# Three direct products for the first batch's maxout, the early loads in one sequence on GpSimd's queue, and a new instruction table

## Chip, core and metric

The kernel runs on one core of a Trainium2 chip. Its time is the device time in microseconds of that core, from launch to the last store. The profile's span is the time from the first to the last instruction of one profiled execution.

## The reference, cut to what matters

Eight batches, eight heads, 576 tokens, head size 64. Each head goes through linear attention with a feature map of 2 x 128 exponentials, and the heads' outputs, side by side, go through a feed-forward layer whose activation is the maximum of three products.

```python
def phi(x):
    proj = np.einsum('bhsd,df->bhsf', x, w_phi)
    proj = proj - np.max(np.abs(proj), axis=-1, keepdims=True)
    return np.concatenate([np.exp(proj), np.exp(-proj)], axis=-1)
q_p, k_p = (phi(q), phi(k))
kv = np.einsum('bhsf,bhsd->bhfd', k_p, v)
z = np.sum(k_p, axis=2)
num = np.einsum('bhsf,bhfd->bhsd', q_p, kv)
den = np.einsum('bhsf,bhf->bhs', q_p, z)[..., None] + 1e-06
x = (num / den)                       # then (tokens, 512)
h = np.maximum(np.maximum(x @ w1, x @ w2), x @ w3)    # 768 wide
out = h @ w_out
```

## The kernel before

**Attention** is cut into 16 units of four heads, two units to a batch, numbered 0 to 15 here. A unit's q and k stand side by side in a bf16 tile `qk_bf` and are transposed into `qkT` (18 tiles of 128 tokens), on TensorE for units 0 to 3 (line 490 for unit 0, line 493 for 1 to 3) and by a transposing DMA from unit 4 on. Then, per unit:

- five groups of projections on TensorE into `psq` and `psk` (L535, L530);
- for k: the exponentials `Ek` on ScalarE (L548), the row maxima `mk` on VectorE (L554), the factor `em` from the maxima (L585), and v times that factor, `vab` (L589), mostly on GpSimd; `kvps` (L643) is the product of the two;
- for q: the row maxima `mqp` on VectorE (L554). In units 0 and 1 the maximum is subtracted inside the product `psm` by small extra matmuls (L616, L619). From unit 2 on the maxima are transposed on TensorE (`pmT`, L562), copied to `mT` and written as one row into `qkT` by a small DMA (L570, from SP or from ScalarE's queue); the product `psm` (L614) waits for that row. The exponentials `Eq` follow on ScalarE (L627);
- `psn` (L661) is the product of `Eq` with the unit's k-v matrix, divided on VectorE (L667, L668) and turned into `xT` (on TensorE for units 0 and 1, L681; by a transposing DMA later).

**The feed-forward layer** takes 512 tokens of each batch as a chunk (chunks 0 to 7), and what is left of all batches as chunk 8. The maximum of three is rewritten: with the weight differences w2-w1 and w3-w1 (the "wd" steps, L785, on GpSimd) a chunk forms max(0, x(w2-w1), x(w3-w1)) from two sets of six `ups` products (four 128x512 matmuls each, L714), and adds x(w1 w_out) as "straight" products (four matmuls to a 128-token tile, L742) into the same accumulators as the down products (six matmuls, L747). w1 w_out is formed once from the transposed w1 (`pwT`, L797; `pm`, L811). The first `ups` set is copied out with a relu on ScalarE (L722) or VectorE (L724), the second is folded in by a maximum on VectorE (L720).

**What sets the order.** Each step is a node with one engine; a table `PLAN` of about 1,470 words fixes the order of the nodes, the engine of each and its buffer slots. A word such as `0G@0.7` is node 0, on GpSimd, ranked at 0.7. The engines run their instructions strictly in that order. The function `fill` puts idle products (`idler`, L842) on TensorE where the table leaves it free in the first stretch.

**Loads.** Unit 0's q and k come over SP's queue in fp32 halves and are cast on ScalarE (L447, L451). Units 1 to 3 take q and k by casting DMAs on GpSimd's queue (L458). The weights are on that queue too (L419), and v on either queue (L472). One-element copies (`gate`, L467) make a later load of v wait for a transposed tile of an earlier unit. A load on GpSimd's queue after the eighth waits for one that was issued eight earlier. `w_phi` is loaded twice, once to each half of the partitions (L360).

## Time and profile before

| | |
|---|---|
| median of 3 runs | 287.12 us (286.9 to 290.07) |
| span of the profiled execution | 285.3 us (no other time is given for it) |
| TensorE busy | 274.8 us, 96% |
| VectorE busy | 208.4 us, 73% |
| ScalarE busy | 192.5 us, 67% |
| GpSimd busy | 125.0 us, 44% |
| mean granted TensorE clock | 0.992 |

Busy shares are means over the whole span; the row of 40 slices and the view by windows show each stretch by itself. A busy TensorE counts a matmul from its start to its modelled end, so neighbours overlap; what a matmul costs in a dense row is the distance between starts. The median lies 1.8 us above the span.

### The profile page before, as it was taken

The page shows a single profiled execution, that of the slowest core. Times are in us where ns is not written, and L with a number is a line of the kernel's source. Part 1 is how long each engine was busy: PE and PEld are TensorE (multiplying, and loading weights), DVE is VectorE, ACT ScalarE, POOL GpSimd, SP SyncE. Part 2 cuts the span into 40 slices and gives each one's busy share as a digit, 9 for nine tenths or more (in the row PEclk, how much of TensorE's full clock was granted, in tenths as well). Part 3 has the DMA queues.
Part 4 walks back from the last instruction along what each step waited for, and adds up shares of the span by engine and source line. Part 5 has one row for each costly group of instructions (what it writes and reads, how often), then busy time and mean ns, then how long its engine had stood idle before and what let it go on. Part 6 is the DMA issues. An engine that isn't in the chain of part 4 may idle for free.

```text
span 285.3 us, 8441 instructions
## 1 busy us (share of the span) xinstructions
PE 274.8 (96%) x3485; PEld 155.7 (55%) x3522; DVE 208.4 (73%) x442; ACT 192.5 (67%) x445; POOL 125.0 (44%) x107
## 2 busy tenths in 40 slices
PE   8889999999999999999999999999999999999995
PEld 3557674565565555456565565555544664444442
DVE  2897899988999868688678779987975472227431
ACT  3798979997999987878868887779775400041001
POOL 9338999945923574417534950160080501000000
PEclk9997999999999999999999999999999999999999
DMA  7999979999899998988897998294420134153135
GB/s 192 203 284 262 312 144 305 341 239 250 221 293 196 225 232 280 251 156 202 258 251 272 268 199 182 99 182 81 82 62 3 27 54 90 37 110 76 37 85 173
DMA packets 67760, 51.46 MB, mean 180 GB/s; under 512 B 48778, under 2 KB 53002, under 8 KB 67722
## 3 DMA queue, kind: packets, MB, share of 16 engines
q1 hardware_dynamic: 62734, 43.38, 60.6%
q0 software_dynamic: 4576, 7.28, 12.1%
q8 instruction: 27, 0.44, 0.6%
q10 hardware_dynamic: 412, 0.28, 0.3%
q14 instruction: 11, 0.09, 0.1%
HBM read 34.67 MB, written 9.44 MB: 155 GB/s over the span
## 4 chain that ended last, share of the span: by engine, by line
PE 81%; DMA 8%; ACT 6%; POOL 1%; DVE 1%; issue 1%; ACTq 0%; POOLq 0%
PE ups L714 29%; PE ops L747 15%; PE ops L742 10%; PE psn L661 6%; PE kvps L643 6%; DMA qk_bf<-in_q_dram 5%; PE psm L614 5%; PE psq L535 4%; DMA qkT<-mT 3%; ACT Eq L627 3%; PE pm L811 2%; ACT Ek L548 2%; PE tps L493 1%; PE psq L530 1%; POOL qk_bf L458 1%
## 5 line engine op out<-in xcount | busy, mean ns | idle before, releaser
L714 PE MATMUL ups<-xT,w_bf 128*128 128x512 bf16 x415 | 101.5, 379 | 1.4 <-ACT Ek L548 0.5
L627 ACT ACTIVATE Eq<-psm 128x512 bf16<-128x512 f32 (+1 forms) x160 | 81.9, 582 | 15.6 <-PE psm L614 12.8
L589 POOL TENSOR_TENSOR vab<-v_raw,em 128x1152 bf16<-128x1152 f32 (+1 forms) x36 | 68.1, 1907 | 36.8 <-ACT em L585 27.9
L548 ACT ACTIVATE Ek<-psk 128x512 bf16<-128x512 f32 x128 | 73.5, 622 | 8.5 <-PE psk L535 5.8
L714 PEld LDWEIGHTS <-w_bf 128*128 128x128 bf16 x432 | 40.6, 98 | 45.4 <-issue 1.0
L720 DVE TENSOR_TENSOR hT<-hT,ups 128x512 bf16<-128x512 bf16 x54 | 36.4, 683 | 24.6 <-ACT hT L722 13.6
L554 DVE TENSOR_REDUCE mqp<-psq 128x4 bf16<-128x512 f32 (+1 forms) x80 | 49.0, 633 | 5.1 <-PE psk L535 2.9
L747 PE MATMUL ops<-wout_bf,hT 128*128 128x512 bf16 (+2 forms) x215 | 51.5, 373 | 0.5 <-issue 0.2
L554 DVE TENSOR_REDUCE mk<-psk 128x4 f32<-128x512 f32 x64 | 43.0, 683 | 0.7 <-PE psk L535 0.5
L747 PEld LDWEIGHTS <-hT 128*128 128x128 bf16 x222 | 21.1, 98 | 23.1
L668 DVE TENSOR_TENSOR x_sb<-psn,rden 128x320 bf16<-128x320 f32 x64 | 31.5, 492 | 2.2
L722 ACT ACTIVATE hT<-ups 128x512 bf16<-128x512 f32 x31 | 18.5, 615 | 21.1 <-PE ups L714 21.0
L755 ACT COPY osb<-ops 128x512 f32<-128x512 f32 (+2 forms) x17 | 9.6, 581 | 30.2 <-PE ops L747 12.7
L661 PEld LDWEIGHTS <-Eq 128*128 128x128 bf16 x640 | 24.9, 97 | 8.0
L755 DVE COPY osb<-ops 128x512 f32<-128x512 f32 x20 | 13.6, 689 | 20.1 <-PE ops L747 18.5
L661 PE MATMUL psn<-kv_sb,Eq 128*128 128x65 bf16 x640 | 26.8, 194 | 0.1
L742 PE MATMUL ops<-xT 128*128 128x512 bf16 x88 | 24.2, 379 | 0.4
L614 PE MATMUL psm<-qkT,wphi_m 128*128 128x512 bf16 (+1 forms) x70 | 22.3, 359 | 0.7 <-DMA qkT<-mT 0.6
L535 PE MATMUL psq<-w,qkT 64*128 64x128 bf16 x256 | 21.5, 217 | 0.5 <-DVE qkT L496 0.2
L476 POOL CAST qk_bf<-q_raw 128x1152 bf16<-128x1152 f32 x12 | 13.8, 1148 | 18.1 <-DMA q_raw<-in_q_dram 9.7
L535 PE MATMUL psk<-w,qkT 64*128 64x128 bf16 x256 | 21.3, 217 | 0.4 <-DVE mqp L554 0.4
L535 PEld LDWEIGHTS <-qkT 64*128 64x128 bf16 x512 | 14.8, 94 | 10.7 <-issue 8.1
(76 smaller groups left out, 272.6 us busy)
## 6 DMA issues: line engine op xcount, KB each, us to landing
out_dram<-osb SPq DMA_DIRECT2D x64, 128.0 KB, 2.5
v_raw<-in_v_dram SPq DMA_DIRECT2D x14, 576.0 KB
k_raw<-in_k_dram SPq DMA_DIRECT2D x11, 576.0 KB, 4.9
q_raw<-in_q_dram SPq DMA_DIRECT2D x11, 576.0 KB, 4.9
w_bf<-in_moe_w_dram POOLq DMA_DIRECT2D x3, 768.0 KB, 11.1
v_raw<-in_v_dram POOLq DMA_DIRECT2D x2, 576.0 KB, 13.7
qk_bf<-in_k_dram POOLq DMA_DIRECT2D x3, 288.0 KB, 13.4
qk_bf<-in_q_dram POOLq DMA_DIRECT2D x3, 288.0 KB, 13.6
```

Of the source, the lines that this page charges most:

```text
L535: nc.tensor.matmul(ps()[:, i, :], lhsT=cols[r, :], rhs=w2[r, c, :], start=True, stop=True)
L548: nc.scalar.activation(Ek[s]()[:, tiles_of(t0, n), :], of(1), EXP, scale=1.0 - 2.0 * s)
L554: nc.vector.tensor_reduce((mq, mk)[c]()[:, tiles_of(t0, n)], of(c), AXX, ALU.max, apply_absolute_value=True)
L589: (nc.vector if n_.eng == "DVE" else nc.gpsimd).tensor_tensor(vab()[:, g, t0:t1, 0:D], vb()[:, t0:t1, :], em()[:, g, t0:t1].unsqueeze(2).t ...
L614: nc.tensor.matmul(psm()[:, 0:w], lhsT=wphi_m, rhs=rhs, start=True, stop=True)
L627: nc.scalar.activation(Eqb()[s][:, cols], psm()[:, 0:w], EXP, scale=1.0 - 2.0 * s)
L661: nc.tensor.matmul(psn()[:, c, :], lhsT=Eqb()[g][:, t0:t0 + P], rhs=kv()[:, pr, ab, g, :], start=(g == 0), stop=(g == 1))
L668: nc.vector.tensor_tensor(x_sb()[:, pr, :, ab, :], psn()[:, :, 0:D], rden().to_broadcast([P, 5, D]), ALU.mult)
L714: nc.tensor.matmul(ups(), lhsT=w_bf[i + 1][:, ct, j * P:(j + 1) * P], rhs=tokens_of(ct), start=(ct == 0), stop=(ct == CT - 1))
L720: nc.vector.tensor_tensor(hT()[:, j, :], hT()[:, j, :], ups(), ALU.max)
L742: nc.tensor.matmul(ops_()[:, 0:width], lhsT=tile_of(ct, tt), rhs=line_w[c_i > MOVE][:, ct, cols], start=(ct == 0), stop=False)
L747: nc.tensor.matmul(ops_()[:, 0:width], lhsT=hT()[:, j, tt * P:(tt + 1) * P], rhs=wout_bf[:, j, cols], start=False, stop=(j == JT - 1))
```

## The change

Five edits, and a table that orders all steps anew.

1. **Chunk 0** takes the maximum of the three direct products x w1, x w2, x w3: eighteen `ups` products instead of twelve, the first six copied out without a relu, the other twelve folded in by a maximum. It has no straight products. The other chunks are as before.
2. **The weight differences** overwrite w2 and w3, so they now wait for chunk 0's products of the same columns, and the second copy of w1 w_out and the gathered last tokens, which overwrite w1, wait for all eighteen.
3. **The early loads** of q, k and v up to unit 3, and q and k of units 4 and 5, are all on GpSimd's queue, except unit 0's q, which stays on SP in two halves. Unit 0's k comes by two casting DMAs. Unit 0's `qk_bf` has the layout of units 1 to 3, so its 18 transposes become 36 half-height ones. The gates are gone.
4. **w_phi** is loaded by one transfer that reads it twice.
5. Some lists of buffers that only served the table lost entries.

The diff, without the table (one row of it stands for the rest):

```diff
-GATES = (None, (0, 0), (1, 0), (2, 0))
 PLAN = """
-0G@0.7 4A@0.7 6S0@0.7 2D0@0.8 3D@1.0 10S0@1.2 1G@1.3 12S@1.6 85G0@1.9 8S@2.1 84G@2.6 1075G@3.3 158G1@4.0 5D@4.1
+2D0@0.7 4A@0.7 6S0@0.7 10G0@0.7 3D@0.8 8S@1.1 83G1@1.4 0G@2.1 82G@2.7 11G@3.4 7D@3.7 1070G@4.2 5D@4.3 13T1@4.5 154G2@4.9
...
-    for ab in range(2):
-        nc.scalar.dma_start(wphi_f[ab * D:(ab + 1) * D, :], w_phi)
+    nc.scalar.dma_start(wphi_f, w_phi.unsqueeze(0).to_broadcast([2, D, DF]))
...
-        qk = buf("qk_bf", QK, [P, 2, UT, D] if by_pe and u else [P, UT, 2 * D], BF16)
+        qk = buf("qk_bf", QK, [P, 2, UT, D] if by_pe else [P, UT, 2 * D], BF16)
...
-                    if u == 0:
-                        def main(what=what, ts=ts, p0=p0, p1=p1, raw=raw):
-                            nc.sync.dma_start(by_pairs(raw()[:, ts, :]), rows_of(what, 0, p0, p1))
...
+                    if u == 0 and what == 0:
+                        def main(ts=ts, p0=p0, p1=p1, raw=raw):
+                            nc.sync.dma_start(by_pairs(raw()[:, ts, :]), rows_of(0, 0, p0, p1))
...
-                if by_pe and u < len(GATES) and GATES[u]:
-                    src, col = units[GATES[u][0]]["qkT"], BATCHES[GATES[u][1]][0] * P
-                    gates.append(nd("gate", {"DVE": 0.1}, lambda src=src, col=col, raw=raw: nc.vector.tensor_copy(
-                        raw()[0:1, 0, 0:1], src()[0:1, col:col + 1]), [], [src, raw]))
-                n_ = nd("Lv" if what == 2 else "L", {"SP": 0.62, "POOL": 0.75} if what < 2 and u <= AHEAD or u < 3 else {"SP": 0.62}, None, gates, [raw],
+                n_ = nd("Lv" if what == 2 else "L", {"POOL": 0.75} if u <= (3 if what == 2 else AHEAD) else {"SP": 0.62}, None, [], [raw],
...
-        for i in range(2):
+        direct = c_i == 0
+        for i in range(3 if direct else 2):
...
-                        nc.tensor.matmul(ups(), lhsT=w_bf[i + 1][:, ct, j * P:(j + 1) * P], rhs=tokens_of(ct),
+                        nc.tensor.matmul(ups(), lhsT=w_bf[i + (not direct)][:, ct, j * P:(j + 1) * P], rhs=tokens_of(ct),
...
-                a = ff(("up", "up2")[i], {"PE": 0.87}, up, ready + [diffs[i][j // 2]], [ups])
+                a = ff(("up", "up2", "up3")[i], {"PE": 0.87}, up, ready + [w_nodes[i] if direct else diffs[i][j // 2]], [ups])
+                if direct:
+                    firsts.append(a)
...
-                    if i == 1:
+                    if i > 0:
                         nc.vector.tensor_tensor(hT()[:, j, :], hT()[:, j, :], ups(), ALU.max)
+                    elif direct:
+                        copy_on[n_.eng](hT()[:, j, :], ups())
...
-                                         start=False, stop=(j == JT - 1))
-                n_s = ff("down", {"PE": 0.87 * width / DM}, straight, ready + lines[c_i > MOVE], [ops_])
+                                         start=(direct and j == 0), stop=(j == JT - 1))
+                n_s = []
+                if not direct:
+                    n_s.append(ff("down", {"PE": 0.87 * width / DM}, straight, ready + lines[c_i > MOVE], [ops_]))
...
+        if b == 1:
+            for i in range(2):
+                for h in range(JT // 2):
+                    diffs[i][h].deps += firsts[(i + 1) * JT + 2 * h:(i + 1) * JT + 2 * h + 2]
+            for n in lines[1]:
+                n.deps += firsts
```

Three places where the order moves. First, the head of GpSimd's queue. Before (the number after `qk_bf` tells the unit: 111 is unit 1, 126 unit 2, 226 unit 3; `k_raw` and `q_raw` here are unit 5's, `v_raw` unit 0's; w1, w2, w3 are `w0_bf`, `w1_bf`, `w2_bf`):

```order
L409 TENSOR_SCALAR minus_72<-ident_70 128x128
L458 DMA qk_bf_111<-in_k_dram 128x2x576
L458 DMA qk_bf_111<-in_q_dram 128x2x576
L419 DMA w0_bf_81<-in_moe_w1_dram 128x4x768
L458 DMA qk_bf_126<-in_k_dram 128x2x576
L458 DMA qk_bf_126<-in_q_dram 128x2x576
L472 DMA v_raw_142<-in_v_dram 128x2x576
L419 DMA wout_bf_84<-in_moe_w_out_dram 128x6x512
L419 DMA w1_bf_82<-in_moe_w2_dram 128x4x768
```

And now (89 is unit 0, 103 unit 1, 147 unit 2, 250 unit 3; `v_raw_180` is unit 0's, `v_raw_219` unit 1's):

```order
L453 DMA qk_bf_89<-in_k_dram 128x576
L453 DMA qk_bf_103<-in_k_dram 128x2x576
masks.py:197 MEMSET ident_69 128x128
masks.py:199 AFFINE_SELECT ident_69<-ident_69 128x128
L453 DMA qk_bf_103<-in_q_dram 128x2x576
L453 DMA qk_bf_89<-in_k_dram 128x576
L414 DMA w0_bf_80<-in_moe_w1_dram 128x4x768
L453 DMA qk_bf_147<-in_q_dram 128x2x576
L414 DMA wout_bf_83<-in_moe_w_out_dram 128x6x512
L462 DMA v_raw_180<-in_v_dram 128x2x576
L404 TENSOR_SCALAR minus_71<-ident_69 128x128
```

Unit 0's k moved here from SP's queue and stands first; the identity and its negative stand behind loads; w2 left the first eight.

Second, ScalarE ahead of chunk 0's first copy-out of `ups`. Before:

```order
L684 COPY xT<-pxT 128x576
L648 CAST kv_sb<-kvps 128x2x130
L815 CAST xT<-pm 128x512
L548 ACTIVATE Ek_721<-psq 128x2x128
L548 ACTIVATE Ek_764<-psk 128x512
L548 ACTIVATE Ek_721<-psk 128x512
L548 ACTIVATE Ek_764<-psq 128x2x128
L585 ACTIVATE em<-mk 128x18 x2
L599 CAST vab<-em 128x36
L548 ACTIVATE Ek_1092<-psk 128x512 x2
L548 ACTIVATE Ek_1106<-psk 128x512 x2
L722 ACTIVATE hT<-ups 128x512 x2
```

And now:

```order
L668 COPY xT<-pxT 128x576 x2
L806 CAST xT<-pm 128x512
L668 COPY xT<-pxT 128x576
L532 ACTIVATE Ek_897<-psk 128x512
L532 ACTIVATE Ek_904<-psq 128x2x128
L532 ACTIVATE Ek_904<-psk 128x512
L532 ACTIVATE Ek_1062<-psk 128x512 x2
L709 CAST hT<-ups 128x512
```

(721 and 764 are unit 2's two tiles of k exponentials before, 897 and 904 now; 1092 and 1106 unit 3's before, 1062 one of them now.) The copy-out now comes before the end of unit 2's exponentials and before unit 2's `em`.

Third, GpSimd between unit 1's `vab` and unit 2's. Before:

```order
L589 TENSOR_TENSOR vab<-v_raw,em 128x9x64 x4
L599 CAST vab<-em 128x2x9
L419 DMA w_bf<-in_moe_w_dram 128x4x768
L785 TENSOR_TENSOR w_bf<-w_bf 128x4x256 x2
L476 CAST qk_bf<-q_raw 128x18x64
L476 CAST qk_bf<-k_raw 128x18x64
L785 TENSOR_TENSOR w_bf<-w_bf 128x4x256
L589 TENSOR_TENSOR vab<-v_raw,em 128x18x64 x2
```

And now (the k load is unit 4's; the first weight load is w2, the second w3):

```order
L462 DMA k_raw_762<-in_k_dram 128x2x576
L414 DMA w1_bf_81<-in_moe_w2_dram 128x4x768
L466 CAST qk_bf_893<-k_raw_391 128x18x64
L462 DMA v_raw_918<-in_v_dram 128x2x576
L466 CAST qk_bf_989<-k_raw_762 128x18x64
L466 CAST qk_bf_989<-q_raw_275 128x18x64
L414 DMA w2_bf_82<-in_moe_w3_dram 128x4x768
L462 DMA v_raw_1064<-in_v_dram 128x2x576
```

The differences left this stretch, and the issue of w3 now stands behind the casts of units 5 and 4.

More of the change, by code (lines that the diff above doesn't have):

```diff
@@ L413 @@
     n_const = node("const", 0, {"DVE": 2.2}, zeros, [n_idle], [])
[L414 removed]
+    n_phi = node("phi", 0, {"ACT": 1.2}, lambda: None, [], [], pipe=0.05, lat=2.0)
     n_phi = node("phi", 0, {"DVE": 0.7}, phi_weights, [n_phi, n_const], [])
@@ L488, in tp @@
                     for n, t in enumerate(range(UT)[tiles_of(t0, nb)]):
-                        if u == 0:
-                            nc.tensor.transpose(tps()[:, n, :], qk()[:, t, :], ident)
-                            continue
                         for c in range(2):
@@ L502, in attention @@
                 tr[i] = c_
-            un["Tc"] = tr
-            for g in gates:
-                g.deps.append(units[GATES[u][0]]["Tc"][GATES[u][1]])
         else:
@@ L539, in attention @@
             a = nd("G", {"PE": 0.22 if n == 2 else 0.236 * len(part)}, lambda mms=mms: [f() for f in mms], [tr[ti], n_phi],
-                   [qkT, mk, mq] + tiles + Ek, mode=int(n == 4))
+                   [qkT] + tiles, mode=int(n == 4))
             projs.append(a)
@@ L644, in kmm @@
                                          start=(t + g == 0), stop=(t == UT - 1 and g == 1))
-        n_k = nd("K", {"PE": KPE}, kmm, exps + n_va, [vab, kv] + kvps + Ek, mode=1)
+        n_k = nd("K", {"PE": KPE}, kmm, exps + n_va, [vab] + kvps + Ek, mode=1)
         for ab in range(2):
@@ L831 @@
             x_last[b // 4][:, :, b % 4 * ST:(b % 4 + 1) * ST], xT[:, b, :, SM:SM + ST]),
-            units[2 * b]["done"] + units[2 * b + 1]["done"] + diffs[0] + diffs[1] + turned, []))
+            units[2 * b]["done"] + units[2 * b + 1]["done"] + diffs[0] + diffs[1] + turned + firsts, []))
     chunk(B, lasts, lambda ct: xT[:, :, ct, SM:SM + ST],
```

316 lines of the change are left out of this document (156 added, 160 removed).

## The prediction

> **What bounds the kernel now.** I read the page first: the busy shares, the 40 slices, the chain.
>
> ```profile
> span 285.3 us, 8441 instructions
> PE 274.8 (96%) x3485; PEld 155.7 (55%) x3522; DVE 208.4 (73%) x442; ACT 192.5 (67%) x445; POOL 125.0 (44%) x107
> PE   8889999999999999999999999999999999999995
> DVE  2897899988999868688678779987975472227431
> ACT  3798979997999987878868887779775400041001
> PE 81%; DMA 8%; ACT 6%; POOL 1%; DVE 1%; issue 1%; ACTq 0%; POOLq 0%
> ```
>
> TensorE is at nine tenths from the fourth slice on and holds 81% of the chain. VectorE and ScalarE are as full as it only in about the first 70 us. So two things count: how much TensorE has to do, and how late the first stretch hands it over. The chain puts chunk 0's first `ups` at 42.86 us, and gives the price of work in dense rows:
>
> ```profile
> 39.87 1.13 PE tps L493 x36
> 42.86 2.54 PE ups L714 x11
> 221.69 3.45 PE ups L714 x16
> 281.95 0.48 ACT osb L755
> ```
>
> A 128x512 product costs 3.45/16 = 0.216 us, a half-height transpose 1.13/36 = 0.031. With such prices for every form, the program's list up to 42.86 us is 25.1 us of work, so TensorE lost 17.7 us there (idle products included). What follows, up to the last product at 281.5, is 232.7 us of work in 238.7: only 6.0 us are lost after 42.86. The windows show who keeps TensorE waiting at first:
>
> ```profile
> 0.00:10.00 10.00, 7.92 (x47) 3.32 (x47) 3.86 (x16) 4.00 (x6) 7.65 (x16) 1.00 0.84 193
> 10.00:20.00 10.00, 8.78 (x160) 6.35 (x161) 9.27 (x21) 9.84 (x25) 2.86 (x5) 1.00 1.16 251
> 9.87:42.86 32.99, 30.94 (x603) 22.45 (x608) 29.57 (x66) 29.43 (x75) 24.08 (x22) 0.95 1.06 245
> 50.00:60.00 10.00, 9.90 (x131) 5.66 (x126) 9.63 (x20) 9.93 (x25) 9.95 (x8) 1.00 1.06 295
> ```
>
> Columns are TensorE, its weight loads, VectorE, ScalarE, GpSimd, granted clock, DMA share, GB/s. From the first exponential (9.87) to the first `ups` VectorE and ScalarE are busy 29.6 and 29.4 of 33.0 us: they set the pace there, and before 9.87 the loads do.
>
> **The change part by part.**
>
> *TensorE's work.* Chunk 0 gains 6 x 4 = 24 `ups` products and loses 4 x 4 = 16 straight ones: 8 x 0.216 = 1.73 us more. In the new order three groups of eight projections that stood ahead of the first `ups` stand behind it: 24 x about 0.03 (the price of the transposes, likewise half-height) = 0.72. So 2.45 us more lie behind the first `ups`. Unit 0's transposes: 36 x 0.031 = 1.1 instead of eighteen, of which eight took 0.61, below: equal.
>
> *The first exponential.* These rows lead up to it:
>
> ```profile
> 1.90 0.94 POOL L458 DMA_DIRECT2D qk_bf<-in_k_dram  x1
> 6.11 0.41 DVE L405 CAST w<-wphi_f 64x128 bf16<-64x128 f32 x1 [2.14 <-DMA wphi_f<-in_w_phi_dram]
> 6.50 0.61 PE L490 MATMUL tps<-ident,qk_bf 128*128 128x128 bf16 x8
> 8.32 1.29 DVE L554 TENSOR_REDUCE mqp<-psq 128x4 bf16<-128x512 f32 x2 [0.49 <-PE psq L535]
> 9.29 0.67 ACT L451 CAST qk_bf<-q_raw 128x576 bf16<-128x576 f32 x1 [0.98 <-DMA q_raw<-in_q_dram]
> 9.72 0.72 POOL L472 DMA_DIRECT2D k_raw<-in_k_dram  x1 [1.65 <-DMA qk_bf<-in_k_dram]
> 11.12 0.73 POOL L472 DMA_DIRECT2D q_raw<-in_q_dram  x1 [0.68 <-DMA qk_bf<-in_q_dram]
> 9.87 4.14 ACT L548 ACTIVATE Ek<-psk 128x512 bf16<-128x512 f32 x8
> ```
>
> ```profile
> q0 software_dynamic: 29, 0.03, 32.5%
> ```
>
> The last row is from the DMA view of the window 5 to 6 us: GpSimd's queue moved its first 29 packets there, and none in the window 0 to 5. The projections were there at 8.3; ScalarE was held by the casts until 9.9. Now everything hangs on unit 0's first half of k, first on GpSimd's queue. Its issue moves from 1.90 to where the identity was filled, 0.72: 1.2 earlier. The first casting load had landed by 9.72 at the latest, the next one 1.4 later, so half a load is 0.7 shorter: at the latest 9.72 - 1.2 - 0.7 = 7.8. Early end: first packet at 5.0 - 1.2, and 0.7 for half a load, 4.5. That queue shared the DMA engines with 1.15 MB on SP's, which is halved now, so I take a value between the ends, 6.5. From the transposes to the first reduction took 8.32 - 6.50 = 1.8, so the exponential comes at 8.4 (ends 6.4, if w_phi lands earlier than at 6.11 too, and 9.7): a gain of 1.4, between 0.2 and 3.4. The second half of q is now cast on ScalarE between exponentials, 0.67, counted below. One w_phi issue less, and the identity behind two issues (0.94 and 0.73), are covered: the table load and the wait for k.
>
> [...]
>
> *ScalarE and VectorE ahead of the first copy-out.* Their groups between 9.87 and 42.86, and from the page the product of two tiles on VectorE:
>
> ```profile
> L548 ACT ACTIVATE Ek<-psk 128x512 bf16<-128x512 f32 x26 | 14.3, 615 | 0.2 <-PE psk L535 0.2
> L554 DVE TENSOR_REDUCE mqp<-psq 128x4 bf16<-128x512 f32 (+1 forms) x14 | 8.4, 627 | 0.2 <-PE psk L535 0.2
> L815 ACT CAST xT<-pm 128x512 bf16<-128x512 f32 x4 | 2.4, 608 | 0.8 <-PE pm L811 0.8
> L684 ACT COPY xT<-pxT 128x576 bf16<-128x576 bf16 x2 | 1.3, 639 | 1.1 <-PE pxT L681 1.1
> ...
> L720 DVE TENSOR_TENSOR hT<-hT,ups 128x512 bf16<-128x512 bf16 x54 | 36.4, 683 | 24.6 <-ACT hT L722 13.6
> ```
>
> An exponential of 512 takes 14.3/26 = 0.55. Counted in the order up to the first `hT<-ups`, ScalarE has four large and two small exponentials fewer (2.2 + 0.8), one `pm` copy (0.6), two `em` and two small copies fewer (0.9); one `kv_sb`, one `pxT` copy and q's cast more (0.4 + 0.6 + 0.7): 2.8 less. VectorE has five large and three small reductions fewer (5 x 0.6 + 3 x 0.35), and `kv_sb`, `pxT`, `mT` and three gates (1.5); q's cast, one `pm` copy and two `vab` products more (0.5 + 0.6 + 1.3, priced as L720): 3.1 less. The two agree on about 2.7, if their idle time stays 3.4 us; 2.0 to 3.0 are the ends. The first `ups` then comes 1.4 + 2.7 = 4.1 earlier, at 38.8 (ends of the gain 2.2 and 6.4).
>
> *Loads behind that.* v of unit 0 has about the same bytes ahead of it as before. GpSimd issues six more loads, 6 x 0.73 = 4.4 us, with room for it (busy 2.86 of 10 us in 10 to 20). Without that cover unit 1's `vab`, its `kvps` and the first `ups` behind them come up to 4.4 later.
>
> *Six more maxima on VectorE* (0.68 each): 4.1 us, in a stretch where it is busy 9.63 of 10. TensorE has 1.73 us more work there; the rest could show, 0 to 2.3. I take 0.3, since reductions stood aside. The differences stay on GpSimd.
>
> *The row of maxima.* From unit 2 on TensorE transposes the maxima, works on, and then stops at `psm` if the row has not landed. By the order, the work between the two is 2.9 us in unit 7 and 3.9 or more elsewhere before; now it is 2.6, 2.7 and 2.6 in units 9, 11 and 13, 3.1 and 3.3 in 7 and 3, 3.7 in 2 and 12. What it takes:
>
> ```profile
> 111.68 0.22 PE L562 MATMUL pmT<-ident,mqp 128*128 128x128 bf16 x1
> 59.92 5.33 DMA qkT<-mT
> 112.22 3.42 DMA qkT<-mT
>   PE psm L614: 0.6, 2
> ```
>
> In unit 7 the row landed at 112.22 + 3.42 = 115.64, 3.96 after the transpose. The last row is from the view of the tile `mT`: two `psm` waited for the row, 0.6 us in all. At 3.96 each, the seven tight units would lose 1.3 + 1.3 + 1.4 + 0.9 + 0.7 + 0.3 + 0.3 = 6.2, less the 0.6 that is in the span already: +5.6. Where the queues are emptier the row needs less, and the loss may be nil: -0.6. Units 9 to 13 come after the first third, when fewer loads stand ahead, so I take +0.3.
>
> **The sum**: -4.1 + 2.45 + 0.3 + 0.3 = -1.05 us, a span of 284.2. The profiled span lies 1.8 under the median of the runs, so the time is 287.1 - 1.05 = 286.1. The difference is a third of a per cent, where a measurement of this kernel tells about 2% from no change.
>
> **The rivals.**
>
> *The whole gain arrives.* -6.4 + 2.45 - 0.6 = -4.55, 282.6. For it: TensorE loses 17.7 us before 42.86, and only there is much to win. Against it: it needs the early end of the load and of each wait. If half of ScalarE's and VectorE's remaining idle 3.4 us went as well, 280.9.
>
> *The row of maxima comes late on the strictly ordered TensorE*, the other side: with the middle start -4.1 + 2.45 + 5.6 = +3.95, 291.1; at worst -2.2 + 2.45 + 5.6 = +5.85, 293.0. It is one mechanism, seven places (`psm` of units 2, 3, 7, 9, 11, 12, 13). It decides once the row takes longer than 3 us from the transpose. For it: 5.33 and 3.42 us of DMA alone. Against it: these two had loads around them.
>
> *w3 lands late.* Its issue now stands behind the casts of unit 4's k and q on GpSimd. Before:
>
> ```profile
> 29.04 2.27 POOL L589 TENSOR_TENSOR vab<-v_raw,em 128x576 bf16<-128x576 f32 x2 [0.15 <-ACT em L585]
> 31.39 0.80 POOL L419 DMA_DIRECT2D w_bf<-in_moe_w_dram  x1
> 36.36 1.15 POOL L476 CAST qk_bf<-q_raw 128x1152 bf16<-128x1152 f32 x1
> w_bf<-in_moe_w_dram POOLq DMA_DIRECT2D x3, 768.0 KB, 11.1
> ```
>
> With unit 1's `vab` done at 31.3 again, two issues, a cast, an issue and two casts that wait for unit 4's k follow: issue at about 37 to 39, landing between 41 (a bare transfer of four) and 50 (the 11.1 us of the page's row). The first product with w3 stands 8.8 us of TensorE's work behind the first `ups`, at 47.6. Price 0 to 2.4: up to 288.5.
>
> *The first exponential does not move* (w_phi and k land as late as k did), and the rest holds: -0.2 - 2.7 + 2.45 + 0.6 = +0.15, 287.3.
>
> *The clock.* Where TensorE had little to do around 18 to 22 us, half the clock was granted:
>
> ```profile
> 20.00:22.00 2.00, 1.55 (x20) 1.12 (x20) 2.00 (x6) 2.00 (x6) 1.54 (x2) 0.88 1.17 269
> 22.00:24.00 2.00, 2.00 (x20) 1.36 (x20) 1.96 (x4) 0.93 (x3) 2.00 (x3) 0.50 1.21 209
> 24.00:26.00 2.00, 2.00 (x37) 1.55 (x33) 1.57 (x4) 1.82 (x6) 1.66 (x2) 0.76 1.16 211
> ```
>
> Now eight idle products instead of seventeen stand ahead of the first transposes. If they run out two us before k lands, the first groups go at half rate: their roughly 2 us of work doubles, +1.7 at most, 287.8. [...]
>
> **How the numbers follow.** Forecast (286.1): 0.36. Whole gain: 0.22. Row late: 0.20. w3 late: 0.12. First exponential unmoved: 0.05. Clock: 0.05. The forecast's own range, by half of each bound, is 284.0 to 288.2. The range for 8 in 10 reaches to 282.0, inside the whole-gain case, and to 291.0, half of the late row's cases. Faster by over 2% (under 281.4): 0.09 of the whole-gain case, where idle time goes too, and 0.03 of the forecast, 0.12. Slower by over 2% (over 292.9): 0.07 of the late row, 0.03 of w3 and of an uncovered GpSimd, 0.10. Within: 0.78.
>
> **What would show it.** First `Ek` at 8.0 to 9.0 and first `ups` at 38 to 40 would show the start right; a first `ups` at 41 or later, wrong. In the chain, `DMA qkT<-mT` at several of the seven units, with TensorE idle before `psm`, would show the late row. A TensorE wait for w_bf near 47 would show w3. Slices of PEclk under 9 in the first four would show the clock. The prediction is wrong if TensorE, after its first `ups`, loses more than 9 us or fewer than 4.

## The result and the profile after

The changed kernel takes 299.33 us (297.58 to 300.26) against 287.32 for the kernel before on the same chip: 1.0404 of it, 95% interval 1.0346 to 1.0462. It is slower. The forecast was 286.1 us, 282 to 291, with 0.78 for "within 2%". The ratios here and below come from undisturbed executions alone and the medians from all of them, so the two need not agree to the last microsecond.

From the page of the changed kernel's profiled execution (the second chain row gives shares by line, the last row is a group of instructions with its busy time, mean duration, and idle time before it with what ended it):

```profile
span 298.4 us, 8521 instructions
PE 280.6 (94%) x3540; PEld 156.6 (52%) x3540; DVE 211.7 (71%) x436; ACT 194.0 (65%) x449; POOL 128.1 (43%) x116
PE   6999999799979999699989979999999999999995
PEclk9999999799999999989999999999999999999999
PE 75%; DMA 13%; DVE 7%; ACT 2%; issue 1%; ACTq 0%; POOLq 0%
PE ups L699 27%; PE ops L736 14%; DMA qkT<-mT 9%; PE ops L731 8%; PE psn L645 6%; PE kvps L627 6%; PE psm L598 5%; PE psq L519 4%; DMA xT<-x_sb 2%; DVE mk L538 2%; DVE mqp L538 2%; DMA qk_bf<-in_k_dram 2%; ACT Ek L532 1%; PE tps L480 1%; PE idler L839 1%
L598 PE MATMUL psm<-qkT,wphi_m 128*128 128x512 bf16 (+1 forms) x70 | 22.1, 371 | 8.9 <-DMA qkT<-mT 8.9
```

DMA has gone from 8% of the chain to 13%, and 9% is one transfer, the row of maxima (`qkT<-mT`): TensorE idles 8.9 us ahead of `psm`, where it idled 0.7 before. In TensorE's row of slices there are now slices of 6 and 7 between the nines. The chain says where (start, duration, what):

```profile
40.18 4.32 PE ups L699 x20
48.91 4.98 DMA qkT<-mT
78.83 5.16 DMA qkT<-mT
84.80 5.37 DMA qkT<-mT
119.66 5.21 DMA qkT<-mT
150.83 3.34 DMA qkT<-mT
168.40 6.65 DMA xT<-x_sb
195.62 2.84 DMA qkT<-mT
```

These are the rows of units 2, 4, 5, 7, 9 and 12, from issue to landing, and one transposing DMA of x. The windows around the first of them (same columns as in the prediction's windows):

```profile
50.00:52.00 2.00, 1.75 (x9) 0.59 (x6) 1.82 (x5) 1.55 (x5) 2.00 (x2) 1.00 1.17 284
52.00:54.00 2.00, 0.06 (x1) 0.07 (x2) 0.21 (x1) 0.64 (x2) 2.00 (x2) 0.98 1.05 387
54.00:56.00 2.00, 2.00 (x5) 0.67 (x6) 0.00 (x0) 1.09 (x2) 0.89 (x1) 0.50 0.29 103
```

TensorE stands still from 51.8 to 53.9 while the DMA engines are full, and once it may go on it runs at half clock: the trace grants 0.5 from 53.90 to 57.31, and again from 125.58 to 128.99 behind unit 7's row.

**Where the 13.1 us went** (298.4 - 285.3), in the prediction's own accounts: the first `ups` is at 40.0 instead of 42.86, -2.8; by the prediction's count 2.45 more TensorE work stands behind it; and behind it TensorE loses 294.8 - 40.0 - 235.2 = 19.6 us instead of 6.0, +13.6; the end behind the last product is 0.2 shorter. These 13.6 are the rows' waits, 8.9 - 0.6 = 8.3; one wait for xT, 1.9; and two windows of 3.41 us at half clock, counted at half of their length each, 3.4. The kernel before also had 0.7 us of other waits behind its first `ups`, and these are gone; so 0.7 of the 13.6 has no place in this list, and the work may have grown by more than the count.

### The profile page after: what moved, and what is told of

It is laid out like the page before. It is cut to its first block, busy times and chain, and to the rows that moved or that the text cites. A ratio compares the mean times of both kernels' runs of the same rounds, so it can differ in the third digit from the quotient of the medians.

```text
span 298.4 us, 8521 instructions
## 1 busy us (share of the span) xinstructions
PE 280.6 (94%) x3540; PEld 156.6 (52%) x3540; DVE 211.7 (71%) x436; ACT 194.0 (65%) x449; POOL 128.1 (43%) x116
## 4 chain that ended last, share of the span: by engine, by line
PE 75%; DMA 13%; DVE 7%; ACT 2%; issue 1%; ACTq 0%; POOLq 0%
PE ups L699 27%; PE ops L736 14%; DMA qkT<-mT 9%; PE ops L731 8%; PE psn L645 6%; PE kvps L627 6%; PE psm L598 5%; PE psq L519 4%; DMA xT<-x_sb 2%; DVE mk L538 2%; DVE mqp L538 2%; DMA qk_bf<-in_k_dram 2%; ACT Ek L532 1%; PE tps L480 1%; PE idler L839 1%
## 5 line engine op out<-in xcount | busy, mean ns | idle before, releaser
L699 PE MATMUL ups<-xT,w_bf 128*128 128x512 bf16 x456 | 107.5, 382 | 2.0 <-DMA xT<-x_sb 1.9
L611 ACT ACTIVATE Eq<-psm 128x512 bf16<-128x512 f32 (+1 forms) x160 | 79.1, 582 | 22.0 <-PE psm L598 21.1
L573 POOL TENSOR_TENSOR vab<-v_raw,em 128x1152 bf16<-128x1152 f32 (+1 forms) x34 | 65.7, 1949 | 44.4 <-ACT em L569 28.7
L699 PEld LDWEIGHTS <-w_bf 128*128 128x128 bf16 x456 | 43.2, 98 | 50.2 <-issue 3.8
L707 DVE TENSOR_TENSOR hT<-hT,ups 128x512 bf16<-128x512 bf16 x60 | 39.7, 683 | 16.4 <-PE ups L699 15.5
L746 ACT COPY osb<-ops 128x512 f32<-128x512 f32 (+2 forms) x24 | 13.7, 585 | 30.4 <-issue 16.2
L713 DVE TENSOR_SCALAR hT<-ups 128x512 bf16<-128x512 f32 x25 | 16.8, 687 | 16.3 <-PE ups L699 16.3
L711 ACT ACTIVATE hT<-ups 128x512 bf16<-128x512 f32 x23 | 13.9, 613 | 19.5 <-PE ups L699 19.4
L627 PE MATMUL kvps<-vab,Ek 64*128 64x65 bf16 x1152 | 21.0, 192 | 0.6 <-DVE xT L806 0.3
L731 PE MATMUL ops<-xT 128*128 128x512 bf16 x80 | 21.3, 392 | 0.0
```

What stands on the lines that cost most here:

```text
L573: (nc.vector if n_.eng == "DVE" else nc.gpsimd).tensor_tensor(vab()[:, g, t0:t1, 0:D], vb()[:, t0:t1, :], em()[:, g, t0:t1].unsqueeze(2).t ...
L611: nc.scalar.activation(Eqb()[s][:, cols], psm()[:, 0:w], EXP, scale=1.0 - 2.0 * s)
L627: nc.tensor.matmul(kvps[ab]()[:, t // NT, g, :], lhsT=Ek[g]()[r, t, :], rhs=vab()[r, g, t, :], start=(t + g == 0), stop=(t == UT - 1 and g ...
L699: nc.tensor.matmul(ups(), lhsT=w_bf[i + (not direct)][:, ct, j * P:(j + 1) * P], rhs=tokens_of(ct), start=(ct == 0), stop=(ct == CT - 1))
L707: nc.vector.tensor_tensor(hT()[:, j, :], hT()[:, j, :], ups(), ALU.max)
L731: nc.tensor.matmul(ops_()[:, 0:width], lhsT=tile_of(ct, tt), rhs=line_w[c_i > MOVE][:, ct, cols], start=(ct == 0), stop=False)
```

## Experiments: the rows of maxima

All times below, but for one that rests on a single execution, are medians of four runs or more, with the ratio to the kernel before on the same chip and its 95% interval. Unless another base is named, an edit is to the changed kernel.

**The control.**

> The changed kernel once more, unaltered, on the chip on which the next three run, so that they have it beside them. Both theories: 1.035 to 1.046 of the kernel before, with the same stalls at psm (about 8 to 11 us together, units 2, 4, 5, 7 the longest).

299.4 us, 1.0473 (1.0438 to 1.0509). The waits for the row were 6.3 us here, and another 1.2 ahead of a `psm` was put down to VectorE; in this execution w3 was late too:

```profile
51.34 0.61 PE L699 MATMUL ups<-xT,w_bf 128*128 128x512 bf16 x2 [1.03 <-DMA w_bf<-in_moe_w_dram]
```

The total repeats; which DMA is the late one differs from one execution to the next.

**Nobody waits for the row.**

```diff
-                qkT()[D:D + 1, :].rearrange("o (t c) -> o t c", c=P), mT())
+                aside[0:UT, :], mT())
```

> The changed kernel, but the row of maxima goes to a small tile of its own, and psm does not wait for it (the subtraction of the maxima is left out from unit 2 on). Theory A (the row comes late on the strictly ordered TensorE): the six stalls of psm, 9.85 us in the changed kernel's trace, go, and with them the two half-clock windows behind the longest of them, 2 x 3.41 us at half rate, some 3.5 us: 299.3 - 13.4 = 286, between 285 and 289, and TensorE loses under 8 us after its first ups. Rival B (the stalls only stand where another shortage shows first, of VectorE, ScalarE or transposing DMAs): under 5 us come back, 294 or more, with new waits ahead of the exponentials or of ups.

294.2 us, 1.033 (1.0254 to 1.0405). This kernel leaves out the subtraction of the maxima from unit 2 on. The stalls at `psm` are gone (0.1 us left in the group), and the traced execution has a span of 289.7, 8.7 under the changed kernel's; but it was the shortest of the four: by the medians 5 us came back and by the ratios 2 to 4, not 13. Theory A's mechanism stood, its sum did not. Rival B was right on the size, but the new waits are no engine's. The view of TensorE's waits (total, times, longest):

```profile
PE ups L700 <- DMA xT<-x_sb: 2.9, 2, 2.7
PE psq L520 <- DMA qkT<-qk_bf: 1.1, 1, 1.1
```

They are other DMAs: the transposing DMA of x at 165.5 us, with a half-clock window of its own behind it (165.86 to 169.28), and the transposing DMA of unit 5's q and k at 63.

**The same in the kernel before.**

> The kernel before with the row of maxima in a tile of its own for which nobody waits (the subtraction of the maxima is left out from unit 2 on). If the order before had the cover that the change lost, the row costs it next to nothing: 0.6 us of waits for the tile mT in its trace, so 0.995 to 1.0 of the kernel before. If rows cost it more than its trace shows (late exponentials behind them), 0.985 to 0.994.

284.75 us, 0.9958 (0.9939 to 0.9977). In the old order the row cost 1.2 us, in the new one 2 to 5. The row is the same transfer in both; what differs is when it is issued, what moves beside it, and how much TensorE work stands between the transpose of the maxima and `psm` (its cover).

**psm moved back in the order.** In the table's order the six units' `psm` and exponentials get 1.4 to 2.9 us on their start, and whatever depends on them or takes their buffers next is moved behind them. The edit also lets no new idle products in behind 13 us; the trace has the same twenty as the changed kernel's.

```diff
+    later = {2: 2.7, 4: 2.2, 5: 1.4, 7: 2.9, 9: 1.6, 12: 1.4}
...
+        if n.kind in ("M", "eq") and n.u in later:
+            n.start += later[n.u]
```

> The changed kernel with the psm products of the six units that stalled (2, 4, 5, 7, 9, 12) and their exponentials 1.4 to 2.9 us later in the order, so that other products stand between the transpose of the maxima and psm; nothing is left out, and the rows' DMAs are as they were. Theory A (what was lost is the cover between transpose and psm): most of the 9.85 us of stalls and the 3.5 of half clock go; 13.4 at best, some of it given back where numerators and x come later: 287 to 292. Rival B (the rows are late because the DMA engines are full, and what comes behind psm is as short of cover): the stalls move to psn or ups, under 4 us gained, 295 or more.

320.1 us, 1.1201 (1.1151 to 1.1251): 20 us worse, which neither theory had. Against the changed kernel's trace the span is 21.2 us longer; TensorE's waits behind the first `ups` grew from 10.8 to 22.8 us, and 20.5 us there are at half clock instead of 6.8. The waits:

```profile
PE psn L668 <- ACT Eq L634: 4.3, 6, 1.4
PE psm L621 <- ACT Eq L634: 3.4, 3, 2.7
PE psk L542 <- ACT Eq L634: 3.1, 3, 1.9
```

TensorE waits for the delayed exponentials of q (`Eq`), 15.5 us in all, and for the row only 0.7: `psn` needs their results, `psm` and `psk` the buffers that they free. Cover was not had here by pushing one step back: the step's followers need the kernel's same eight `bank` buffers and the same ScalarE.

**Every row from SyncE's queue.**

```diff
+        if n.kind == "V":
+            n.eng = "SP"
```

> The changed kernel with every row of maxima issued from SyncE's queue; five were issued from ScalarE's (units 2, 4, 5, 6, 7: 4.98, 5.16, 5.37, 1.90, 5.20 us from issue to landing, against 1.93 to 3.60 from SyncE's). Theory A1 (the rows wait behind loads and transposes at the DMA engines, whatever queue issues them): rows of units 2, 4, 5, 7 still take 4 us or more, time within 2 us of the changed kernel's, 297 to 301. Theory A2 (it is ScalarE's queue that is served late): they take 2 to 3.5 us, the stalls of these four units (7.8 us) and the half-clock windows (3.5) go: 288 to 291.

307.35 us, 1.065 (1.057 to 1.0731), the wrong side of both theories. Unit 2's row took 4.94 us from this queue as well, so the queue is not what makes it long. Units 4, 5 and 7 took 3.4 to 4.5, but those of 2, 4 and 7 were issued 1.7 to 3.2 us later behind their transposes:

```profile
116.78 7.66 SPq L495 DMA_TRANSPOSE qkT<-qk_bf  x1
127.89 0.81 SPq L557 DMA_DIRECT2D qkT<-mT  x1
L601 PE MATMUL psm<-qkT,wphi_m 128*128 128x512 bf16 (+1 forms) x70 | 22.5, 377 | 13.1 <-DMA qkT<-mT 13.1
```

The issue of a transposing DMA held SyncE for 7.66 us, until 124.44; then four more issues stood ahead of unit 7's row, which was transposed at 124.18, issued at 127.89 and landed at 131.26.

**What makes a row long.** The DMA view between issue and landing in the changed kernel, of the rows of units 2, 5, 7 and, last, 6:

```profile
DMA packets 2224, 1.58 MB, mean 315 GB/s; under 512 B 1761, under 2 KB 1761, under 8 KB 2224
DMA packets 997, 2.12 MB, mean 392 GB/s; under 512 B 87, under 2 KB 87, under 8 KB 996
DMA packets 2615, 1.15 MB, mean 222 GB/s; under 512 B 2379, under 2 KB 2379, under 8 KB 2614
DMA packets 128, 0.03 MB, mean 16 GB/s; under 512 B 128, under 2 KB 128, under 8 KB 128
```

The first three took 4.98, 5.37 and 5.21 us, the last 1.90. Large loads (unit 5) and the many small packets of a transposing DMA (unit 7) do it alike. In the first 4.0 us behind the issue of unit 2's row no packet of ScalarE's queue starts, and then all 27 do within 0.1 us; in units 5 and 7 the first starts after 4.0 and 4.3 us, in unit 6 after 1.4, and only unit 4's are spread, from 2.0 to 4.6. The row's first completion, 1.1 to 1.8 us after the issue in all fourteen, comes ahead of its packets in these five and says nothing of its data. So these rows were late to begin, not slow to move: but for unit 4's, all 27 packets of a row started within 0.9 us. The next experiment takes the loads away from ahead of three rows:

```diff
+        if n.kind == "V" and n.u in (2, 4, 5):
+            n.eng = "SP"
+        if n.eng == "SP" and n.kind in ("L", "Lv"):
+            for a, row in ((39.0, 45.2), (69.9, 70.8), (71.0, 75.3)):
+                if a < n.start < row:
+                    n.start = row + 0.01 * (1 + n.start - a)
```

> The changed kernel with the rows of units 2, 4 and 5 on SyncE's queue and the loads of k, q and v that stood just ahead of them there moved behind them (two ahead of unit 2's row, one ahead of unit 4's, three ahead of unit 5's). In the changed kernel 1.56, 1.58 and 2.11 MB were moved between the issue of these rows and their landing, 4.98, 5.16 and 5.37 us; unit 6's row, with 0.02 MB beside it, took 1.90. If the bytes ahead of a row set its length, the three take 2 to 3 us, their stalls (2.35, 1.88, 1.04 us) fall under 0.5 each and the half-clock window behind the first (1.7 us) goes: 5 to 6 us less, 293 to 295. If loads that come later make units late instead, TensorE waits for transposing DMAs (qkT<-qk_bf) and the time is 297 or more with rows as short.

296.2 us, 1.0282 (1.0208 to 1.0357). The three rows took 2.04, 2.23 and 2.07 us instead of 4.98, 5.16 and 5.37, and their stalls are gone; beside unit 4's 0.61 MB were moved instead of 1.60. On SyncE's queue with the loads still ahead the same rows had taken 4.94, 3.87 and 4.52: here it was the bytes ahead that made these rows long, not the queue. The time fell by 3 us by the medians and 5 by the ratios. Both branches of the expectation came true in part, since other DMAs are now late (TensorE's waits):

```profile
PE psq L527 <- DMA qkT<-qk_bf: 1.7, 1, 1.7
PE ups L707 <- DMA xT<-x_sb: 1.6, 2, 0.9
PE psm L606 <- DMA qkT<-mT: 1.4, 3, 0.6
```

The same kernel on another chip:

> The kernel with rows first once more, unaltered, on the chip of the next two. Where it is the DMAs that land at other times from one execution to the next, it is again between 1.02 and 1.036 of the kernel before, with rows of 2 to 2.3 us in units 2, 4 and 5 and TensorE waiting for other DMAs (unit 5's transposing DMA at 65 us, xT at 106 and 167).

296.66 us, 1.0352 (1.0288 to 1.0416); rows of 3.12, 2.24 and 1.93 us, and 2.5 us of waiting for unit 5's transposing DMA, but none for xT. By this one rows first gains 1.5 to 3.5 us, depending on which ratio of the changed kernel it is held against. The waits change places again.

## Experiments: what else is late

**w3 earlier on GpSimd's queue.**

```diff
+        if n.kind == "W" and n.u == 2:
+            n.start = 29.25
```

> The changed kernel with w3's load issued on GpSimd's queue right behind w2's, ahead of the casts of unit 4; in the changed kernel it was issued at 38.42, as the transposing DMA of unit 4 began, which took SyncE 9.26 us instead of 2.80, and as unit 2's row was to go. If w3 beside the transposing DMA is what delays unit 2's row (4.98 us), that row lands in 2 to 3 us, the stall of 2.35 us and the half-clock window behind it (1.7 us) go, and the time falls by 3 to 4, 295 to 296. If not (the row is late through its queue or the other loads), the stall at psm of unit 2 stays over 1.5 us and the time within 1 us of 299.3.

299.47 us, 1.0386 (1.0281 to 1.0492): nothing gained. Unit 2's row did take 2.83 us and did not stop TensorE, as the first branch had it; the 2.8 us that TensorE was ahead at 60 us were all but gone at 90:

```profile
PE psm L602 <- DMA qkT<-mT: 7.8, 5, 3.1
PE psq L523 <- DMA qkT<-qk_bf: 1.8, 1, 1.8
```

Unit 5's transposing DMA stopped it at 66.2, and the rows of units 5 and 7 took 6.37 and 5.99 us.

**The weight differences left out**, with the row aside. A guess of mine was that GpSimd, where 12.7 us of differences now stand behind 51 us instead of ahead of 52, hands over its casts late.

```diff
-            n_ = node("wd", 0, {"DVE": 1.2, "POOL": 2.1}, None, [w_nodes[0], w_nodes[i + 1]], [])
-            n_.fn = lambda n_=n_, f=diff: f(n_)
+            n_ = node("wd", 0, {"DVE": 1.2, "POOL": 2.1}, lambda: None, [w_nodes[0], w_nodes[i + 1]], [])
```

> As the kernel with the row aside (nobody waits for the row of maxima, their subtraction is left out from unit 2 on), and the six weight differences on GpSimd (2.1 us each, 12.7 us, since the change behind chunk 0's products instead of between 32 and 52 us) are left out too. With the row aside the time was 1.033 of the kernel before, and TensorE then waited for a transposing DMA at 63 us (1.28), vab of GpSimd at 149.7 (0.97), xT at 165.5 (2.88 and a half-clock window). If the late differences hold up GpSimd's casts and with them the transposing DMAs, the first of these goes and the time falls by 2 to 4 us against the row aside: 1.02 to 1.026. If not, it stays within 1 us of it, and what is left of the loss lies in xT and in small waits.

297.2 us, 1.0318 (1.0231 to 1.0405), as with the row aside alone. The guess falls: without any differences unit 5's transposing DMA was as late.

```profile
PE psq L520 <- DMA qkT<-qk_bf: 2.1, 1, 2.1
```

**Loads behind unit 5's transposing DMA**, on top of rows first:

```diff
-            for a, row in ((39.0, 45.2), (69.9, 70.8), (71.0, 75.3)):
+            for a, row in ((39.0, 45.2), (50.0, 51.8), (69.9, 70.8), (71.0, 75.3)):
```

> The kernel with rows first, and the two loads ahead of unit 5's transposing DMA on SyncE's queue (1.15 MB) moved behind it. In the kernel with rows first TensorE waited 1.84 us for that DMA at 65 us. If it lands late because of the loads ahead of it, the wait falls under 0.5, and the time by 1 to 2 us against rows first (by 3 in executions with a half-clock window behind it). If the transposes themselves take that long, or the x of units 2 and 3 behind them come late instead, it is within 1 us.

294.4 us, 1.0287 (1.0224 to 1.035), 2.3 us under rows first on the same chip, though the intervals overlap. The wait at 65 us is gone, as expected. What is left in the traced execution:

```profile
PE ups L707 <- DMA xT<-x_sb: 4.3, 3, 2.2
PE psm L606 <- DMA qkT<-mT: 3.4, 5, 2.0
```

**More loads moved back and w3 early**, on top of rows first:

```diff
+        if n.kind == "W" and n.u == 2:
+            n.start = 29.25
+    first = sorted(n.start for n in order if n.eng == "SP" and n.kind in ("X", "V"))
+    for n in sorted((n for n in order if n.eng == "SP" and n.kind in ("L", "Lv")), key=lambda n: n.start):
+        for row in first:
+            if 80.0 < row and row - 2.5 < n.start < row:
+                n.start = row + 0.01 * (1 + n.start - row + 2.5)
+                break
```

> The kernel with rows first (1.028 of the kernel before), and in the same way one load put behind the transposing DMA of unit 9's x, and two behind the rows of units 11 and 12; w3's load is issued right behind w2's. If what is left of the loss lies in DMAs that land behind loads, the wait for xT near 167 us (0.92 there, 2.0 in the changed kernel) goes, and the executions in which w3 was late (1.2 us at 51 us) too: 291 to 293, 1.015 to 1.024. It should not come under the kernel before: 1.8 us more TensorE work and the wait for unit 5's transposing DMA at 65 us (1.84) stay, against a start that is 2 to 3 us earlier. If the remaining loss is elsewhere (VectorE, ScalarE), 1.025 or more.

296.6 us, 1.0342 (1.0271 to 1.0413): no better than rows first. The wait for xT near 167 went and came back at 110.9, 2.3 us, and unit 5's transposing DMA cost 2.2, each with a half-clock window behind it.

**Half the bytes.** So far each experiment moved one late transfer and another took its place. This one thins out all of them and leaves the order alone; from unit 6 on only half of each q and k is loaded.

```diff
+                p1 = 1 if what < 2 and u >= 6 else 2
+                n_.fn = lambda n_=n_, what=what, raw=raw, p1=p1: queue_of[n_.eng].dma_start(
+                    by_pairs(raw()[:, 0:NT * p1, :]), rows_of(what, u, 0, p1))
```

> The changed kernel with half of each load of q and k from unit 6 on (288 instead of 576 KB; the casts read that half twice, and the results are not the reference's). The order is as in the changed kernel, and so is every engine's work but two casts for one on GpSimd. If the bytes in flight make the rows and xT late, the rows of units 2, 4 and 5 take 2.5 to 4 us instead of 5.0 to 5.4, xT at 175 us no longer stops TensorE, and 5 to 8 us of the 13 come back: 291 to 294, 1.018 to 1.03. If the rows take as long with half the bytes, it is the cover in the order alone: 1.037 or more.

292.4 us, 1.0217 (1.0158 to 1.0275): 5 to 7 us back by the ratios, the most of all. Behind the start no half-clock window is left; the rows of units 4, 5 and 7 took 3.51, 4.71 and 3.09 us. Unit 2's, which has the transposing DMA of unit 4 beside it, stayed at 5.05. TensorE's waits:

```profile
PE psm L605 <- DMA qkT<-mT: 1.7, 4, 0.7
PE ups L706 <- DMA xT<-x_sb: 1.7, 1, 1.7
PE ups L706 <- DMA w_bf<-in_moe_w_dram: 1.4, 1, 1.4
```

> The kernel before with the same halved loads of q and k from unit 6 on (the casts read one half twice, the results are not the reference's). The changed kernel gained 7 us by this (1.0473 to 1.0217 of the kernel before). If that gain came from transfers that land late on an order without cover, the order before, which has the cover, gains next to nothing: 0.992 to 1.0. If fewer bytes help any order as much (VectorE's or ScalarE's reads and writes going faster, or units coming earlier), it gains like the changed kernel, 0.97 to 0.98.

284.5 us, 0.9927 (0.99 to 0.9954). The same halving is worth 2.1 us in the old order and 5 to 7 in the new. The old order is nearly indifferent to how fast the transfers are, the new one is not: that difference, 3 to 5 us, is the cost of late transfers on an order without cover, and the 4.8 us of waits still in the fence above belong to it too.

## Experiments: the clock and the start

**Idle products in the waits.** The edit was to put eight idle products ahead of the first `psm` of units 2 and 7.

```diff
+                    if u in (2, 7) and ch.start == 0 and ts.start == 0:
+                        for _ in range(8):
+                            nc.tensor.matmul(psm(), lhsT=idle, rhs=idle.unsqueeze(1).to_broadcast([P, 4, P]),
+                                             start=True, stop=True)
```

> The changed kernel with eight idle products (1.73 us at full clock) ahead of the first psm of units 2 and 7, where TensorE waits 2.35 and 2.49 us for the row and then ran a window of 3.41 us at half clock. If the waits bring the half clock, both windows go, and the time falls by 2 x 1.7 = 3.4 us less what the idle products overrun the waits: 296 to 298, 1.035 of the kernel before. If the granted clock does not hang on the waits, the windows stay and the time is 299 to 301.

300.4 us, 1.0491 (1.0424 to 1.0558). The test missed its place: the edit hung on the `psm` of the first group of columns, which in both units is not the first in the order, so TensorE idled 1.95 and 1.63 us as before and the products came later. In this execution no half-clock window followed, so the price of the windows was not tested this way. The traces give it all the same. Take from each span the start of the first `ups`, TensorE's waits behind it, and half of the time at half clock behind it (all in us):

| traced execution | span | first `ups` | waits | half of half clock | what is left |
|---|---|---|---|---|---|
| kernel before | 285.3 | 42.9 | 1.3 | 0 | 241.1 |
| changed kernel | 298.4 | 40.0 | 10.8 | 3.4 | 244.2 |
| every row from SyncE's queue | 304.0 | 40.0 | 14.9 | 5.1 | 244.0 |
| rows first | 290.2 | 40.5 | 5.2 | 0 | 244.5 |
| half the bytes | 290.0 | 41.0 | 4.8 | 0 | 244.3 |

In the new order what is left agrees within 0.5 us here, and without the clock's column it would differ by 5: a window cost about 1.7 us here. The kernel with the idle products leaves 248.0, of which the sixteen products (0.216 each) are 3.5. Against the kernel before the rest grew by 3.1 us, the waits by 9.5 and the clock's part by 3.4, with 2.8 gained at the start: that is the whole difference between the two spans.

**More idle products at the start.**

```diff
-SLOW = 4.6
+SLOW = 1.0
```

> The changed kernel with 13 instead of 8 idle products ahead of unit 0's first transposes. In the changed kernel the clock was half until 9.53 us: the first transposes came at 6.35 as forecast, but from there to the first reduction it took 3.04 us against 1.8 in the kernel before, with three idle products at half rate in between (1.46 us). With the clock full from about 4.5 us that should take 1.8 to 2.1, and the first exponential come 2.6 to 3 us behind the first transposes instead of 3.8; the first ups 0.5 to 1 us earlier if ScalarE's start carries through, unmoved if loads set it.

The time of its one execution was 300.4 us. The changed kernel's start first (TensorE, then VectorE's first reduction and ScalarE's first exponential), then this kernel's:

```profile
1.04 3.60 PE L839 MATMUL idler<-idle 128*128 128x512 bf16 x8 [1.04 <-DVE idle L407]
6.35 1.06 PE L480 MATMUL tps<-ident,qk_bf 128*64 128x128 bf16 x15 [1.47 <-DMA qk_bf<-in_k_dram]
7.35 1.46 PE L839 MATMUL idler<-idle 128*128 128x512 bf16 x3
9.39 0.69 DVE L538 TENSOR_REDUCE mk<-psk 128x4 f32<-128x512 f32 x1 [1.25 <-PE psk L519]
10.11 1.79 ACT L532 ACTIVATE Ek<-psk 128x512 bf16<-128x512 f32 x3 [6.90 <-DVE mk L538]
```

```profile
1.04 4.32 PE L839 MATMUL idler<-idle 128*128 128x512 bf16 x13 [1.04 <-DVE idle L407]
6.60 0.63 PE L480 MATMUL tps<-ident,qk_bf 128*64 128x128 bf16 x15 [1.07 <-DMA qk_bf<-in_k_dram]
7.17 0.82 PE L839 MATMUL idler<-idle 128*128 128x512 bf16 x3
8.46 0.69 DVE L538 TENSOR_REDUCE mk<-psk 128x4 f32<-128x512 f32 x1 [0.50 <-PE psk L519]
9.19 1.08 ACT L532 ACTIVATE Ek<-psk 128x512 bf16<-128x512 f32 x2 [5.96 <-DVE mk L538]
```

With five more idle products the clock was full from 3.80 us instead of 9.53. The same fifteen transposes then take 0.63 instead of 1.06 us, the three idle products that stand ahead of the projections 0.82 instead of 1.46, and from the first transposes to the first exponential it takes 2.6 us instead of 3.8, as expected. The first `ups` came at 40.10 all the same; a wait of 1.2 us at 37.1 took the place of the gain. One execution does not show that the five products did it: with eight, six of thirteen traced executions had the full clock from 3.7 to 5.4 us too, and five of these lost it again between 7.1 and 8.7.

## Why the prediction was wrong, step by step

**The row of maxima: the step that failed.** The term was +0.3 with ends -0.6 and +5.6; it measured +8.3 in the waits, and with the two half-clock windows behind them, for which the sum had no term, +11.7. Its mechanism was one of the rivals, its size was not in any. I took one duration, 3.96 us from the transpose (the row at 112.22), as the dear case for every unit and compared it with the cover of each. Measured from the transpose, units 2, 4, 5 and 7 took 6.1, 6.4, 5.9 and 5.75 us, and units 3, 6, 11 and 13 2.4 to 2.6. So the list of seven units was wrong as well: it followed the cover alone, and missed units 4 and 5, with 4.6 and 4.9 us of cover, while units 3, 11 and 13, which were on it, lost nothing. The row at 59.92, 5.33 us, stood in the prediction, and I set it aside because "these two had loads around them". That was the whole point: that row took its 5.33 us with 1.5 MB beside it, and the new order had 1.2 to 2.1 MB beside four rows. That the loads would be fewer was right from unit 8 on, where 1.8 us of waits remained.

**No term for the transfers as a class.** The prediction priced one transfer with thin cover. xT (1.9), unit 5's transposing DMA (1.1 to 2.5 in several executions) and w3 (0.8 to 1.4 in some) had no term or a small rival each. From 49 to 54 us, while unit 2's row was under way in the changed kernel, the packets of SyncE's queue (q1) took 106.8% of the 16 DMA engines' span by the DMA view, and those of the row's (q10) 0.5%. The experiments show that these transfers stand in for each other: taking one away gave back 0 to 5 us, thinning all of them 5 to 7. The bare transfer of four at the early end for w3 was an estimate; its load took 10.5 us from issue to landing in the changed kernel's trace.

**The first exponential.** Forecast 8.4, measured 10.11, no gain. The k half landed at about 6.3 as assumed (6.5), so the load was right; the 1.8 us behind it became 3.0 to the first reduction, with the clock half until 9.53 us in this execution and eight idle products ahead instead of seventeen. That was the clock rival, with a chance of 0.05 and nearly the right size (1.2 us of the 1.7); TensorE stood idle 1.47 us ahead of the transposes, and the rival's two was an estimate. In most executions of the new order with eight idle products the last window at half clock ended between 9.5 and 13 us.

**ScalarE and VectorE ahead of the first copy-out.** The 2.7 us were about right: from the first exponential to the first `ups` it took 29.9 us, before 33.0; in the fourteen traced executions with the new order 29.7 to 31.0. So the first `ups` came 2.8 earlier, not 4.1.

**TensorE's work**, +2.45, was about right: the table of spans leaves 3.1, and nothing here shows where the 0.7 between them lies. **Six more maxima**: +0.3 was not tested by itself; the 1.2 us put down to VectorE in one execution may belong here, and this stays open.

**The tests that I set** were right as tests but for one: the first `ups` at 40.0 said the start was nearly as forecast, `DMA qkT<-mT` came up in the chain, and 19.6 us lost behind the first `ups` was far over the bound of 9. The one for the clock could not show: the PEclk slices are nines from the start, though three idle products took 1.46 us at 7.35 (0.82 with thirteen idle products ahead of the transposes), since the trace's record of the clock begins at 9.53.

**What stays open.** Medians of the kernels with rows first or aside lie 3 to 5 us above their traced executions, so part of their loss is in no trace here. With the row aside the clock accounts for some of it: 0.992 was granted in the traced execution and 0.977 to 0.986 in the others, 1.7 to 4.4 us of 290. With rows first it does not (0.994 traced, 0.989 to 1.000). How the rows' cost splits between shorter cover and more traffic is only bounded: the two act together.

## What to carry to other kernels

A transfer's duration in a trace held for its surroundings: in the changed kernel the same row took 1.90 us with 0.03 MB beside it and 5.37 with 2.12. Before an order is changed, find the longest one of its kind, ask what moved beside it, and price the new order with that wherever loads or transposing DMAs will stand next to it, not with the usual one. Ask of an order how much work of the bounding engine stands between each issue and the first use: here an order that saved 2.8 us at the start and cost 3 in work lost 13 in waits and half clock, by leaving less of it than the slow transfers need. Where waits for several transfers are close behind each other, removing one can show what the next one costs (with the row aside, 2.7 us for xT and 1.1 for unit 5's transposing DMA); thin out all of them (half the bytes, 5 to 7 us here) to see the sum.

## What the runs showed of the chip

- A row of 18 x 128 values took 1.8 to 2.3 us in all traces with under 0.05 MB moved between its issue and its landing, and 3.1 to 6.4 with 1.0 to 2.3 MB, from either queue.
- In these traces the granted clock changed on a fixed grid of 3.41 us: the half-clock windows at 53.90 and 125.58 in the changed kernel start 21 such steps apart, those at 21.54 and 284.36 in the kernel before 77, those at 55.74, 86.46 and 130.83 with every row on SyncE's queue 9 and 13. In the fourteen traces of the new order, behind the first 13 us, all sixteen full-clock steps in which TensorE idled for 2.07 us or more were followed by half clock, none with less than 1.68, and 4 of the 13 in between. In the changed kernel the steps from 50.49 and 122.17, with 2.15 us (of unit 2's wait of 2.19) and 2.32 us idle, had half clock behind them, those from 81.21 and 173.37, with 1.72 each, had not. A wait of 3.1 us with w3 early had none behind it: it ended at 126.95, and the edge at 125.11 lies inside it. No bound holds for both orders: in the kernel before, the step from 18.12 had 1.30 us idle and half clock behind it.
- Issuing a transposing DMA of q and k held SyncE for 2.6 to 10.0 us over the traces (2.71 to 5.50 in the kernel before, 2.63 to 9.26 in the changed one; unit 4's 2.80 and 9.26), with everything queued behind it.
